# A linear-attention block with two MLPs on one core: the bonus moves from a transposed product to the diagonal of the score tile

## The chip, the cores and the metric

The program runs on one core of a Trainium2 chip. The metric is the device time of one execution in microseconds (us); lower is better. In the profile PE is TensorE's matmuls, PEld its weight loads (each matmul needs one, and they run beside the matmul before them), DVE is VectorE, ACT is ScalarE, POOL is GpSimd, and SP issues the DMA transfers.

## The reference

Four batches of eight heads run a recurrence with a decaying state over 768 steps, and the result goes through two MLPs of width 384 to 2048 to 384.

```python
for t in range(S):                       # S = 768, D = 48
    kt, vt, rt, wt = (k[:, :, t], v[:, :, t], r[:, :, t], w[:, :, t])
    cur = np.einsum('bhd,bhe->bhde', u[None] * kt, vt)
    y[:, :, t] = np.einsum('bhd,bhde->bhe', rt, state + cur)
    state = wt[:, :, :, None] * state + np.einsum('bhd,bhe->bhde', kt, vt)
...
h = x @ w_in;  y1 = (h * np.clip(h + 3.0, 0.0, 6.0) / 6.0) @ w_out
h = y1 @ w_in2;  out = (h / (1.0 + np.exp(-h))) @ w_out2
```

Step t reads the state of the steps before it, and of itself only the "bonus": v at t times the sum over d of r*u*k at t. So in a tile of scores between 128 steps and 128 steps, the entries above the diagonal are decayed products of r and k, and the bonus sums belong on the diagonal.

## The kernel before

**Work.** The sequence is cut into six chunks of 128 steps; a *group* is one chunk of one batch, 24 in all (j is the chunk, g the group). Each group passes through `attention`: VectorE makes running products of the decay forwards and backwards (`pre`, `suf`, lines 600 and 607, with a small reciprocal at 603 between them) and scales r and k by them (`rh`, `kh`, lines 612 and 615). TensorE makes two score tiles `pa` (line 625), each 128 by 4 by 128 for four pairs of heads, and VectorE copies them to SBUF times the mask `causal` (line 636, `a`). `causal` is one above the diagonal and zero on and below it. TensorE also transposes `kh` (line 646, `pk`), ScalarE copies that (650, `khn`), and TensorE makes the chunk's addition to the state (741, `pkv`), which ScalarE or VectorE adds and decays (767; 758 and 759).

**The bonus.** For the groups of the first chunk, VectorE multiplies r by k (line 655, `rkp`) and TensorE sums over d (662, `bb`); for later groups GpSimd makes the products (667 and 670, `ruk`) and VectorE sums them (674). Then `bonus` multiplies v by these sums: three VectorE instructions at lines 685 and 689 into the tile `bv` (the same memory as `ruk`). TensorE adds `bv` to the output in PSUM by three transposing matmuls against the identity (718), after the products of state and scores with r and v (704). ScalarE copies the output `py` to `x` (727).

**MLP blocks.** `block1` and `block2` run per chunk over 16 slices of the hidden width: three groups of products into `h` (821 or 831), an activation, and three groups into an accumulator (842 or 851). Block 0 uses plain f32 products with weights in `val`, which VectorE unpacks from 64-bit words in three steps (32, 38 and 44); the others use f32r products of high and low parts. Attention of chunk j+1 is interleaved with block1 of chunk j.

**Order.** All operations are collected in a `Plan` with a cost in ns for each engine that may run them and a key. `Plan.order` walks through them in planned time, puts next on each engine what can start first, and among equals the lowest key. What comes out is a fixed order for each engine; only semaphores decide the real times. An operation with `port=True` shares one planned resource with GpSimd. `keep_busy` adds products of the identity that nobody reads (`filler`, line 572) with the highest key, so that the plan puts them where TensorE has nothing else to do before the MLPs: 10 pairs planned at 430 ns and 60 at 215 ns.

Of the kernel before, what the change touches and what calls it, by code (L numbers as in the profile page):

```python
# [10 lines left out]
I32 = mybir.dt.int32  # L11
# [333 lines left out]
def tile_decay_attention_mlp2(  # L345
# [109 lines left out]
    def load_w(layer, fc, key, where="wp", after=(), whole=False):  # L455
# [14 lines left out]
        if WW == 2:  # L470
            op({"DVE": 580}, key, lambda e: upper_bits(e, raw.ap, val.ap.bitcast(I32)), [raw], [val])
            for step in (sign_bits, lower_bits):
                op({"DVE": 960}, key, lambda e, step=step: step(e, raw.ap, val.ap.bitcast(I32)),
                   [raw, val], [val], port=True)
# [103 lines left out]
    keep_busy(10, 430)  # L578
    keep_busy(60, 215)
# [8 lines left out]
    def attention(g, key):  # L588
# [14 lines left out]
        op({"DVE": 150}, key, lambda e: e.reciprocal(  # L603
# [8 lines left out]
        op({"DVE": 690}, key, lambda e: e.tensor_tensor(  # L612
            rh.ap, of(rk, 0, NP), pre.ap[:, :, 0:C], op=ALU.mult
        ), [rk, pre], [rh], port=True)
        op({"DVE": 690}, key, lambda e: e.tensor_tensor(
# [14 lines left out]
        o_scores = op({"PE": 900}, key, scores, [kh, rh], pa)  # L630
        if g == 2:
            first_scores.append(o_scores)
        a_sb = []
        for i in range(2):
            a = att("a", [128, NP, C], g, str(i), bufs=2)
            op({"DVE": 690}, key, lambda e, a=a, pa=pa[i]: e.tensor_tensor(  # L636
                a.ap, pa.ap, causal.ap.unsqueeze(1).to_broadcast([128, NP, C]), op=ALU.mult
            ), [pa[i], causal], [a])
            a_sb.append(a)

        if not last:
# [6 lines left out]
            op({"PE": 350}, key, back, [kh, ident], [pk])  # L648
# [3 lines left out]
        ruk = att("ruk", [128, H, D], g)  # L652
        if first:
            rkp = att("rkp", [PD, NP, C], g)
            op({"DVE": 690}, key, lambda e: e.tensor_tensor(
# [9 lines left out]
            op({"PE": 900}, key, sums, [rkp, u_bd], [bb])  # L665
        else:
            op({"POOL": 1000}, key, lambda e: e.tensor_tensor(  # L667
# [9 lines left out]
        bv = Part(ruk.buf, lambda t: flat(ruk).rearrange("p (c a e) -> p c a e", c=KC, e=Q))  # L677
        bv.writes, bv.reads = ruk.writes, ruk.reads

        def bonus(e):  # L680
            b = bb.ap.rearrange("p (a i) x -> p a i x", i=2)
            x = vn.ap.rearrange("p a (n t) -> p a n t", t=T)
            n = Q // T
            for k in range(n):
                e.tensor_tensor(
                    bv.ap[:, 0:2, :, k * T:(k + 1) * T].rearrange("p c a e -> p a c e"),
                    x[:, :, k::n + 3, :], b.to_broadcast([128, NP, 2, T]), op=ALU.mult,
                )
# [402 lines left out]
```

## Time and profile before

| what | value |
|---|---|
| median of three runs | 931.77 us (931.74 to 931.96) |
| profiled execution, its own time | 932.04 us |
| its span, first to last instruction | 930.0 us |
| PE, PEld busy | 922.3 us, 725.1 us |
| DVE, ACT, POOL busy | 575.3 us, 269.3 us, 47.5 us |
| first product of an MLP starts at | 38.40 us |

Busy shares are means over stages. Until 38.40 us the four groups of the first chunk run alone; after that products of the MLPs fill TensorE, and attention of the other twenty groups lies between them until about 441 us. PE's busy time counts products that overlap, and its ends are modelled; whether TensorE waits is better read from the waits and from the spacing of its weight loads.

### The profile page before, as it was taken

To read this page: it belongs to the slowest core of one execution; us is meant where nothing else is said; L and a number is where in the kernel's file an instruction comes from. 1 tells how busy PE (TensorE), PEld (TensorE's weight loads), DVE (VectorE), ACT (ScalarE), POOL (GpSimd) and SP (SyncE) were. 2 spreads that over 40 slices of the span, in tenths; PEclk is the share of its full clock that TensorE was granted. 3 is DMA by queue.
4 is the path that set the end of the run, shared out by engine and by line. 5 is a ranking of instruction groups with operands and counts; after the bars stand their busy time and mean duration, and the time that the engine had idled before them with its cause. 6 is when DMAs were issued, how large, how long until landed. Compare 5 with 4: busy or idle time off the path is not lost.

```text
span 930.0 us, 13728 instructions
## 1 busy us (share of the span) xinstructions
PE 922.3 (99%) x5638; PEld 725.1 (78%) x5638; DVE 575.3 (62%) x998; ACT 269.3 (29%) x496; POOL 47.5 (5%) x52
## 2 busy tenths in 40 slices
PE   9999999999999999999999999999999999999997
PEld 7655457888888888888888888888888888888886
DVE  7998888886676768575449878644543632322221
ACT  2311423222221222121126865422322321211111
POOL 1110001100110010110000000000000000000000
PEclk9999999999999999999999999999999999999999
DMA  9566523321321223120057675554744500100101
GB/s 282 160 206 201 176 57 102 97 74 56 93 58 58 92 68 97 32 88 1 1 193 216 194 228 190 200 174 136 237 136 136 181 23 0 35 1 1 35 0 36
DMA packets 39603, 101.12 MB, mean 109 GB/s; under 512 B 3696, under 2 KB 16112, under 8 KB 39536
## 3 DMA queue, kind: packets, MB, share of 16 engines
q1 hardware_dynamic: 39536, 100.20, 34.1%
q8 instruction: 45, 0.74, 0.3%
q14 instruction: 22, 0.18, 0.1%
HBM read 90.75 MB, written 9.44 MB: 108 GB/s over the span
## 4 chain that ended last, share of the span: by engine, by line
PE 99%; ACT 0%; POOL 0%; issue 0%; POOLq 0%
PE h L831 39%; PE acd L851 21%; PE acc L851 18%; PE h L821 5%; PE acc L842 4%; PE py L704 4%; PE pa L625 3%; PE filler L572 2%; PE py L718 1%; PE pk L646 1%; PE pkv L741 1%; PE bb L662 0%; ACT o L927 0%; ACT x L727 0%; POOL ident masks.py:199 0%
## 5 line engine op out<-in xcount | busy, mean ns | idle before, releaser
L831 PE MATMUL h<-x,w 128*128 128x512 f32 x1584 | 392.6, 391 | 0.0
L831 PEld LDWEIGHTS h<-x,w 128*128 128x128 f32 x1584 | 295.9, 188 | 61.4 <-issue 0.5
L851 PE MATMUL acd<-gh,w 128*128 128x512 f32 x576 | 192.8, 389 | 0.0
L862 DVE CAST gh<-g 128x512 fp32r<-128x512 f32 x146 | 62.5, 428 | 201.0 <-ACT g L921 197.6
L851 PE MATMUL acc<-gh,w 128*128 128x512 f32 x480 | 163.9, 392 | 0.0
L921 ACT ACTIVATE g<-h 128x512 f32<-128x512 f32 x96 | 57.4, 598 | 264.8 <-PE h L831 243.2
L882 ACT ACTIVATE g<-h 128x512 f32<-128x512 f32 x96 | 57.4, 598 | 237.2 <-PE h L831 188.5
L851 PEld LDWEIGHTS acd<-gh,w 128*128 128x128 f32 x576 | 108.1, 188 | 22.4
L864 DVE TENSOR_TENSOR gl<-g,gh 128x512 fp32r<-128x512 f32 x176 | 121.4, 690 | 5.0 <-ACT gh L861 0.8
L884 DVE SCALAR_TENSOR_TENSOR g<-g,h 128x512 f32<-128x512 f32 x96 | 65.9, 686 | 82.5 <-ACT g L882 82.2
L851 PE MATMUL acd<-gl,w 128*128 128x512 f32 x288 | 112.0, 389 | 0.0
L851 PEld LDWEIGHTS acc<-gh,w 128*128 128x128 f32 x480 | 90.1, 188 | 19.1
L851 PE MATMUL acc<-gl,w 128*128 128x512 f32 x240 | 93.5, 390 | 0.0
L851 PEld LDWEIGHTS acd<-gl,w 128*128 128x128 f32 x288 | 54.1, 188 | 11.3
L851 PEld LDWEIGHTS acc<-gl,w 128*128 128x128 f32 x240 | 45.1, 188 | 9.0
L821 PE MATMUL h<-x,val 128*128 128x512 f32 x96 | 44.8, 597 | 0.6 <-ACT x L727 0.6
L842 PE MATMUL acc<-g,val 128*128 128x512 f32 x96 | 43.8, 592 | 0.0
L667 POOL TENSOR_TENSOR ruk<-rkn,u_bc 128x384 f32<-128x384 f32 x20 | 21.0, 1051 | 377.8 <-PE py L718 316.8
L842 PEld LDWEIGHTS acc<-g,val 128*128 128x128 f32 x96 | 17.9, 190 | 21.0 <-issue 19.9
L821 PEld LDWEIGHTS h<-x,val 128*128 128x128 f32 x96 | 17.5, 190 | 19.6 <-issue 18.7
L802 DVE TENSOR_SCALAR_CACHE_REDUCE cval<-cval 128x768 f32<-128x768 f32 x32 | 30.3, 946 | 2.3 <-ACT cval L28 2.3
L636 DVE TENSOR_TENSOR a<-pa,causal 128x512 f32<-128x512 f32 x42 | 27.1, 685 | 7.3 <-PE pa L625 7.3
(106 smaller groups left out, 730.8 us busy)
## 6 DMA issues: line engine op xcount, KB each, us to landing
raw<-in_moe_w_dram SPq DMA_DIRECT2D x32, 768.0 KB, 4.7
craw<-in_moe_w_dram SPq DMA_DIRECT2D x32, 768.0 KB, 4.4
rk<-in_rk_dram SPq DMA_DIRECT2D x21, 448.0 KB, 4.0
rkn<-in_rkn_dram SPq DMA_DIRECT2D x20, 384.0 KB, 3.3
cw<-in_wseq_dram SPq DMA_DIRECT2D x24, 226.2 KB, 2.9
ws<-in_wseq_dram SPq DMA_DIRECT2D x22, 226.2 KB, 2.8
vn<-in_vn_dram SPq DMA_DIRECT2D x22, 224.0 KB, 2.6
x2d<-x SPq DMA_DIRECT2D x18, 256.0 KB, 2.2
```

The source lines that it names most:

```text
L625: e.matmul(pa[i].ap[:, p, :], kh.ap[rows, p, :], rh.ap[rows, p, :], start=True, stop=True,)
L704: e.matmul(py.ap[p * Q:(p + 1) * Q, c, :], lhs, rhs, start=p not in begun, stop=False, skip_group_check=True,)
L802: op({"DVE": 600}, key, lambda e: e.tensor_scalar(val.ap, val.ap, TINY, 0.0, op0=ALU.is_lt, op1=ALU.add, accum_out=stray.ap[:, col:col + 1 ...
L821: op({"PE": 860}, key, lambda e, kc=kc: e.matmul(h.ap, wh.ap[:, 0, kc * 128:(kc + 1) * 128], xh.ap[:, kc, :], start=kc == 0, stop=kc == KC ...
L831: e.matmul(h.ap, a.ap[:, 0, kc * 128:(kc + 1) * 128], b.ap[:, kc, :], start=(kc == 0 and i == 0), stop=(kc == KC - 1 and i == 2),)
L842: op({"PE": 860}, key, lambda e, c=c: e.matmul(acc[c].ap, wh.ap[:, 1, c * 128:(c + 1) * 128], gh.ap, start=fc == 0, stop=fc == FC - 1,), [ ...
L851: e.matmul(acc[c].ap, a.ap[:, 1, sl], b.ap, start=(fc == 0 and i == 0), stop=(fc == FC - 1 and i == 2),)
L862: else e.tensor_copy(gh.ap, src.ap)
L864: op(lo_engs, key, lambda e: e.tensor_tensor(gl.ap, src.ap, gh.ap.bitcast(F32), op=ALU.subtract), [src, gh], [gl], port=True)
L882: op({"ACT": 595}, kk, lambda e, g=g, h=h: e.activation(g.ap, h.ap, AF.Relu, bias=3.0), [h], [g])
L884: op({"DVE": 690}, kk, lambda e, g=g, h=h: e.scalar_tensor_tensor(g.ap, g.ap, 6.0, h.ap, op0=ALU.min, op1=ALU.mult), [g, h], [g])
L921: op({"ACT": 595}, kk, lambda e, g=g, h=h: e.activation(g.ap, h.ap, AF.Silu), [h], [g])
```

## The change

The bonus sums go on the diagonal of the score tile. ScalarE first fills `a` with the identity scaled by the sums, four activations of 128 by 128 for each of the two tiles (`diagonal`); VectorE then copies the scores over it where the mask is not zero (`copy_predicated`) in place of the multiplication by the mask. The product of `a` with v then contains the bonus. The tile `bv`, its three VectorE instructions and the three transposing matmuls of each group are gone. For the first four groups the sums lie in PSUM, and a small activation copies them to SBUF (`bs`); their product and sum get a slightly lower key. The planned costs of several operations are changed, and the filler is 16 pairs planned at 430 ns and 24 at 300 ns.

```diff
-    keep_busy(10, 430)
-    keep_busy(60, 215)
+    keep_busy(16, 430)
+    keep_busy(24, 300)
...
-        for i in range(2):
-            a = att("a", [128, NP, C], g, str(i), bufs=2)
-            op({"DVE": 690}, key, lambda e, a=a, pa=pa[i]: e.tensor_tensor(
-                a.ap, pa.ap, causal.ap.unsqueeze(1).to_broadcast([128, NP, C]), op=ALU.mult
-            ), [pa[i], causal], [a])
...
-            op({"DVE": 690}, key, lambda e: e.tensor_tensor(
+            op({"DVE": 600}, key - 0.05, lambda e: e.tensor_tensor(
                 rkp.ap, of(rk, 0, NP), of(rk, 1, NP), op=ALU.mult
             ), [rk], [rkp], port=True)
...
-        def bonus(e):
...
-        op({"DVE": 880}, key, bonus, [vn, bb], [bv], port=not first)
+        if first:
+            bs = Part(new("ap", "bs", 2, [128, H, 1], f"bs{g}"))
+            op({"ACT": 200}, key, lambda e: e.activation(flat(bs), flat(bb), AF.Copy), [bb], [bs])
+        else:
+            bs = bb
+        a_sb = []
+        for i in range(2):
+            a = att("a", [128, NP, C], g, str(i), bufs=2)
+
+            def diagonal(e, a=a, i=i):
+                for p in range(NP):
+                    e.activation(a.ap[:, p, :], ident.ap, AF.Copy, scale=bs.ap[:, 2 * p + i])
+
+            op({"ACT": 1000}, key, diagonal, [bs, ident], [a])
+            op({"DVE": 610}, key, lambda e, a=a, pa=pa[i]: e.copy_predicated(
+                a.ap, causal.ap.bitcast(I32).unsqueeze(1).to_broadcast([128, NP, C]), pa.ap
+            ), [pa[i], causal], [a])
+            a_sb.append(a)
...
-            for c in range(KC):
-                e.matmul(
-                    py.ap[:, c, :], bv.ap[:, c].rearrange("p a e -> p (a e)"), ident.ap,
-                    start=False, stop=True, is_transpose=True, skip_group_check=True,
-                )
...
-        op({"PE": 1950 if state else 1300}, key, outputs,
-           [*a_sb, vn, bv, ident] + ([rh, state] if state else []), [py])
+        op({"PE": 1700 if state else 1050}, key, outputs,
+           [*a_sb, vn] + ([rh, state] if state else []), [py])
```

The orders move in several places. First VectorE in the opening stage. The names `spare` and `home` are tiles of the first groups kept in space that weights take later; `spare_0_...` holds `pre` and `suf`, `spare_1_...` holds `rh` and `kh`, `spare_2_...` holds `a` and `rkp`. Before, from the start of the fourth group's `pre` to its `rkp`:

```order
L600 SCALAR_TENSOR_TENSOR spare_0_413<-homews,ind 112x516
L685 TENSOR_TENSOR spare_1_357<-home_144,bb_406 128x4x2x16 x2
L689 TENSOR_TENSOR spare_1_357<-home_144,bb_406 128x128
L636 TENSOR_TENSOR spare_2_393<-pa_2_415,causal 128x512
L636 TENSOR_TENSOR spare_2_393<-pa_2_417,causal 128x512
L603 RECIPROCAL indq<-spare_0_413 112x4
L612 TENSOR_TENSOR spare_1_478<-home_159,spare_0_413 112x512
L607 SCALAR_TENSOR_TENSOR spare_0_413<-homews,indq 112x516
L655 TENSOR_TENSOR spare_2_510<-home_159 112x512
L615 TENSOR_TENSOR spare_1_478<-home_159,spare_0_413 112x512
L747 COPY grown_528<-spare_0_413 112x4
```

And in the changed kernel, from the same `pre` to the first step of the second weight slice:

```order
L600 SCALAR_TENSOR_TENSOR spare_0_377<-homews,ind 112x516
L603 RECIPROCAL indq<-spare_0_377 112x4
L612 TENSOR_TENSOR spare_1_398<-home_161,spare_0_377 112x512
L646 TENSOR_TENSOR spare_2_405<-home_161 112x512
L683 COPY_PREDICATED spare_2_316<-causal,pa_2_379 128x512
L683 COPY_PREDICATED spare_2_316<-causal,pa_2_381 128x512
L607 SCALAR_TENSOR_TENSOR spare_0_377<-homews,indq 112x516
L734 COPY grown_469<-spare_0_377 112x4
L32 TENSOR_SCALAR val_0_471<-raw_0_173 128x768
L615 TENSOR_TENSOR spare_1_398<-home_161,spare_0_377 112x512
L38 SCALAR_TENSOR_TENSOR val_0_471<-raw_0_173,val_0_471 128x768
L32 TENSOR_SCALAR val_0_471<-raw_1_175 128x768
```

The three bonus instructions are gone, the two instructions on the scores of the third group stand behind `rkp` of the fourth instead of ahead of its `rh`, and the second unpacking step of the first weight slice (38) has moved ahead of the last scores.

Second, VectorE from the last score copies of the opening stage to the first activation of MLP block 0 (`g_0`), which TensorE needs for its first accumulation. Before:

```order
L636 TENSOR_TENSOR spare_2_510<-pa_3_533,causal 128x512
L636 TENSOR_TENSOR spare_2_510<-pa_3_535,causal 128x512
L38 SCALAR_TENSOR_TENSOR val_0_530<-raw_0_172,val_0_530 128x768
L38 SCALAR_TENSOR_TENSOR val_0_530<-raw_1_178,val_0_530 128x768
L44 SCALAR_TENSOR_TENSOR val_0_530<-raw_0_172,val_0_530 128x768
L44 SCALAR_TENSOR_TENSOR val_0_530<-raw_1_178,val_0_530 128x768
L600 SCALAR_TENSOR_TENSOR pre_617<-ws_433,ind 112x516
L674 TENSOR_REDUCE bb_623<-ruk_543 128x8
L603 RECIPROCAL indq<-pre_617 112x4
L612 TENSOR_TENSOR rh_626<-rk_441,pre_617 112x512
L607 SCALAR_TENSOR_TENSOR suf_632<-ws_433,indq 112x516
L884 SCALAR_TENSOR_TENSOR g_0_630<-g_0_630,h_0_0_615 128x512
```

In the changed kernel (line 871 is the old 884):

```order
L683 COPY_PREDICATED spare_2_405<-causal,pa_3_486 128x512
L683 COPY_PREDICATED spare_2_405<-causal,pa_3_488 128x512
L38 SCALAR_TENSOR_TENSOR val_0_471<-raw_1_175,val_0_471 128x768
L600 SCALAR_TENSOR_TENSOR pre_568<-ws_407,ind 112x516
L44 SCALAR_TENSOR_TENSOR val_0_471<-raw_1_175,val_0_471 128x768
L32 TENSOR_SCALAR val_2_575<-raw_2_519 128x768
L603 RECIPROCAL indq<-pre_568 112x4
L612 TENSOR_TENSOR rh_580<-rk_411,pre_568 112x512
L38 SCALAR_TENSOR_TENSOR val_2_575<-raw_2_519,val_2_575 128x768
L607 SCALAR_TENSOR_TENSOR suf_588<-ws_407,indq 112x516
L44 SCALAR_TENSOR_TENSOR val_2_575<-raw_2_519,val_2_575 128x768
L871 SCALAR_TENSOR_TENSOR g_0_586<-g_0_586,h_0_0_571 128x512
```

Before, four unpacking steps, all of the first weight slices (`val_0`), and the sum `bb_623` stand between the last score copies and `g_0`. Now five steps stand there, two of `val_0` and three of the next pair of slices (`val_2`), and the sum has moved behind `g_0`.

Third, TensorE at the output of the first group of the second chunk. Before:

```order
L741 MATMUL pkv_697<-vn_447,khn_676 48x48 x8
L704 MATMUL py_708<-rh_626,s_111 32x128 x12
L704 MATMUL py_708<-a_4_682,vn_447 32x128 x4
L704 MATMUL py_708<-a_4_689,vn_447 32x128 x4
L704 MATMUL py_708<-a_4_682,vn_447 32x128 x4
L704 MATMUL py_708<-a_4_689,vn_447 32x128 x4
L718 MATMUL py_708<-ident,ruk_543 128x128 x3
L821 MATMUL h_0_3_745<-x_0_0_287,val_2_639 128x512 x3
```

In the changed kernel:

```order
L808 MATMUL h_0_3_673<-x_0_0_281,val_2_575 128x512 x2
L728 MATMUL pkv_680<-vn_422,khn_675 48x48 x8
L696 MATMUL py_690<-rh_580,s_111 32x128 x12
L696 MATMUL py_690<-a_4_618,vn_422 32x128 x4
L696 MATMUL py_690<-a_4_632,vn_422 32x128 x4
L696 MATMUL py_690<-a_4_618,vn_422 32x128 x4
L696 MATMUL py_690<-a_4_632,vn_422 32x128 x4
L808 MATMUL h_0_3_673<-x_0_0_281,val_2_575 128x512
```

The three transposing products are gone, and nothing else in the piece differs but the place in the MLP block at which it stands. Over the whole program the attention pieces between MLP products number 46 before and 43 in the changed kernel (the product of the last check not counted); the commonest output piece was `pkv` then `py` (10 times) and is now `py` then `pkv` (8 times, and 3 times behind a `pk`).

## Rows read from the trace of the kernel before

**Rows 1.** The page's chain that ended last, shares of the span by engine.

```profile
PE 99%; ACT 0%; POOL 0%; issue 0%; POOLq 0%
```

**Rows 2.** All of TensorE's waits: line, releaser: us in total, times, longest.

```profile
PE filler L572 <- POOL ident masks.py:199: 1.4, 1, 1.4
PE h L821 <- ACT x L727: 0.6, 1, 0.6
```

**Rows 3.** Timeline of VectorE over one opening group: start, duration, instruction, [idle before].

```profile
8.91 1.23 DVE L600 TENSOR_TENSOR_SCAN spare<-ws,ind 112x516 f32<-112x516 f32 x1
...
17.93 0.48 DVE L685 TENSOR_TENSOR spare<-vn,bb 128x128 f32<-128x128 f32 x2 [0.91 <-PE bb L662]
19.01 1.29 DVE L636 TENSOR_TENSOR spare<-pa,causal 128x512 f32<-128x512 f32 x2 [0.40 <-PE pa L625]
...
20.30 0.66 DVE L612 TENSOR_TENSOR spare<-home,spare 112x512 f32<-112x512 f32 x1
...
20.88 1.23 DVE L607 TENSOR_TENSOR_SCAN spare<-homews,indq 112x516 f32<-112x516 f32 x1
...
22.02 0.67 DVE L655 TENSOR_TENSOR spare<-home 112x512 f32<-112x512 f32 x1
...
22.61 0.69 DVE L615 TENSOR_TENSOR spare<-home,spare 112x512 f32<-112x512 f32 x1
...
23.28 1.23 DVE L600 TENSOR_TENSOR_SCAN spare<-homews,ind 112x516 f32<-112x516 f32 x1
```

**Rows 4.** The same timeline where GpSimd works beside VectorE.

```profile
27.78 1.39 POOL L667 TENSOR_TENSOR ruk<-rkn,u_bc 128x384 f32<-128x384 f32 x1 [24.45 <-DVE indq L603]
...
28.23 2.03 DVE L607 TENSOR_TENSOR_SCAN spare<-homews,indq 112x516 f32<-112x516 f32 x1
...
30.18 1.42 DVE L655 TENSOR_TENSOR spare<-home 112x512 f32<-112x512 f32 x1
```

**Rows 5.** Timeline of the end of the opening stage, all engines.

```profile
32.19 1.02 DVE L32 TENSOR_SCALAR val<-raw 128x768 int32<-128x768 int32 x2
...
33.91 1.29 DVE L636 TENSOR_TENSOR spare<-pa,causal 128x512 f32<-128x512 f32 x2
...
35.12 1.82 DVE L38 SCALAR_TENSOR_TENSOR val<-raw,val 128x768 int32<-128x768 int32 x2
35.45 0.56 PE L741 MATMUL pkv<-home,spare 128*48 128x48 f32 x16
...
36.26 1.08 PE L704 MATMUL py<-spare,home 128*32 128x128 f32 x32
...
37.86 0.49 ACT L727 ACTIVATE x<-py 128x384 f32<-128x384 f32 x1
38.40 5.42 PE L821 MATMUL h<-x,val 128*128 128x512 f32 x12 [0.58 <-ACT x L727]
```

**Rows 6.** Timeline of the first activation and the first accumulation of block 0.

```profile
41.98 0.66 DVE L884 SCALAR_TENSOR_TENSOR g<-g,h 128x512 f32<-128x512 f32 x1
...
43.66 1.88 PE L842 MATMUL acc<-g,val 128*128 128x512 f32 x4
```

**Rows 7.** Weight-load timeline at an output piece of block 1.

```profile
390.63 0.31 PEld L718 LDWEIGHTS py<-ident,ruk 128*128 128x128 f32 x3 [0.20 <-issue]
390.91 0.19 PEld L851 LDWEIGHTS acc<-gh,w 128*128 128x128 f32 x1
```

**Rows 8.** Timeline of ScalarE: eight small activations scaled per partition, from PSUM.

```profile
21.20 1.73 ACT L767 ACTIVATE s<-pkv,grown 48x48 f32<-48x48 f32 x8 [1.11 <-PE pkv L741]
```

**Rows 9.** Windows of filler's weight loads: stretch, its length, busy (count), PEclk, DMA share, GB/s.

```profile
2.00:7.00 5.00, 3.51 (x24) 1.00 0.94 265
7.60:9.20 1.60, 1.43 (x16) 1.00 1.01 297
```

**Rows 10.** Weight-load timeline of one opening group, `bb` to the next filler.

```profile
16.83 0.97 PEld L662 LDWEIGHTS bb<-u_bd,spare 112*128 112x128 f32 x8
...
19.26 1.07 PEld L572 LDWEIGHTS <-ident 128*128 128x128 bf16 x10
```

More of the change, by code (lines that the diff above doesn't have):

```diff
@@ L470, in load_w @@
         if WW == 2:
-            op({"DVE": 580}, key, lambda e: upper_bits(e, raw.ap, val.ap.bitcast(I32)), [raw], [val])
+            op({"DVE": 480}, key, lambda e: upper_bits(e, raw.ap, val.ap.bitcast(I32)), [raw], [val])
             for step in (sign_bits, lower_bits):
-                op({"DVE": 960}, key, lambda e, step=step: step(e, raw.ap, val.ap.bitcast(I32)),
+                op({"DVE": 870}, key, lambda e, step=step: step(e, raw.ap, val.ap.bitcast(I32)),
                    [raw, val], [val], port=True)
@@ L602, in attention @@
         ), [ws, ind], [pre], port=True)
-        op({"DVE": 150}, key, lambda e: e.reciprocal(
+        op({"DVE": 100}, key, lambda e: e.reciprocal(
             indq.ap[:, 1:SEQ + 1].rearrange("p (a b) -> p a b", b=SEG)[:, :, C:SEG],
@@ L628, in scores @@
                     )
-        o_scores = op({"PE": 900}, key, scores, [kh, rh], pa)
+        o_scores = op({"PE": 1090}, key, scores, [kh, rh], pa)
         if g == 2:
             first_scores.append(o_scores)
-        a_sb = []
-        for i in range(2):
-            a = att("a", [128, NP, C], g, str(i), bufs=2)
-            op({"DVE": 690}, key, lambda e, a=a, pa=pa[i]: e.tensor_tensor(
-                a.ap, pa.ap, causal.ap.unsqueeze(1).to_broadcast([128, NP, C]), op=ALU.mult
-            ), [pa[i], causal], [a])
-            a_sb.append(a)
         if not last:
@@ L663, in sums @@
                              start=True, stop=True)
-            op({"PE": 900}, key, sums, [rkp, u_bd], [bb])
+            op({"PE": 790}, key - 0.05, sums, [rkp, u_bd], [bb])
         else:
+            ruk = att("ruk", [128, H, D], g)
             op({"POOL": 1000}, key, lambda e: e.tensor_tensor(
@@ L676, in attention @@
             ), [ruk], [bb])
-        bv = Part(ruk.buf, lambda t: flat(ruk).rearrange("p (c a e) -> p c a e", c=KC, e=Q))
-        bv.writes, bv.reads = ruk.writes, ruk.reads
-        def bonus(e):
[L681 to L687, printed above, removed]
-                )
-            e.tensor_tensor(
-                bv.ap[:, 2].rearrange("p a (i e) -> p a i e", i=2),
-                x[:, :, n:n + 3:2, :], b.to_broadcast([128, NP, 2, T]), op=ALU.mult,
-            )
-        op({"DVE": 880}, key, bonus, [vn, bb], [bv], port=not first)
+        if first:
[14 more added lines that the diff above has]
+            a_sb.append(a)
         state = states.get(o)
```

8 lines of the change are left out of this document (3 added, 5 removed).

## The prediction

> **What bounds the kernel now.** I read the chain of what ended last first: nearly all of it is TensorE [rows 1]. That alone could be a model's artefact, so the list of TensorE's waits comes next. It has two entries: 1.4 us before the first filler product, and 0.6 us before the first MLP product [rows 2]. After 38.4 us TensorE never waits for another engine, so there a product taken out of its order is time gained and work of the others is hidden. The timeline of the opening stage shows the other regime. There TensorE is busy with filler that nobody reads, and VectorE sets the pace: one group takes it from one `pre` to the next, with waits of 0.91 us (for `bb`) and 0.40 us (for the scores) in it [rows 3]. So the kernel has two parts with different bounds: VectorE's chain up to 38.4 us, TensorE's order after it.
>
> A caution on the first reading. The Trainium skill (Perfetto Trace Analysis, section "Identifying the Most-Contended Engine") says that matmul busy time is a bad measure of TensorE's headroom and that the busy share of the weight loads should be taken. Here that share is 725.1 of 930.0 us, 78%; by that rule a fifth of TensorE is free, the removed products could have been hidden, and the sum below would lose its first term and give about 927.8 us. The waits of this trace do not bear it out: the idle time of a weight load ends with "issue", when the product before it is through [rows 7], and not with another engine.
>
> **The change, part by part.**
>
> *Transposes removed from TensorE.* At an output piece in block 1 the three weight loads of the transposes begin at 390.63 us and the next MLP load at 390.91: 0.28 us [rows 7]. Twenty groups lie after the opening: 20 x 0.28 = 5.6 us. If the 0.20 us of idle ahead of them went too it would be 9.6 us, but I expect such a pause at the new seam, where `py`'s narrow products meet a full-width load. The order also joins pieces differently (43 for 46), which I value at nothing, with 1 us either way. Term 1: -5.6 us (-4.6 to -6.6).
>
> *The opening stage, VectorE.* Per group, from the starts in rows 3: `pre` 1.23, the score pair and the reciprocal 1.29 (19.01 to 20.30), `rh` 0.58, `suf` 1.14, `rkp` 0.59, `kh` with the small copy 0.67; together 5.50 us. The bonus and the waits around it, 2 us more a group, are what disappears: `bb` is now made earlier and feeds ScalarE, and the scores are asked for two instructions later than they were. The second `pre` starts at 8.91 us [rows 3] behind the same seven instructions, reordered. To the last group's score copies there are then three groups' worth, 16.5 us; two first unpacking steps at 0.51 and two others at 0.91 (half of 1.02 and of 1.82) [rows 5], 2.84 us, of which only the 1.02 stood ahead of them before; and the stretch while GpSimd works, where `suf` took 2.03 for 1.23 us and `rkp` 1.42 for 0.67 [rows 3, 4], 1.55 us. GpSimd starts there when its data lands, so I leave it in the same place, though other instructions will meet it. Sum: 8.9 + 20.9 = 29.8 us, against 33.91 [rows 5].
>
> From there to the MLP: the copies 1.29; `py` right behind them (before, `pkv` and filler put it at 36.26, 1.06 after the copies ended); from `py` to `x` 1.60 less the transposes' 0.28; from `x` to the first MLP product 0.54 [rows 5]. That is 33.0 us against 38.4. Term 2: -5.4 us. Without the GpSimd stretch it is -6.9; with one more us of seams -4.4.
>
> *Price of the predicated copy.* The trace shows none. Below, it costs what the masked multiplication does, 0.60 us apiece in the pair above; above, two cycles an element as in the scan, 1.23 us [rows 3]. It reads the same PSUM tile and mask and writes the same tile as the multiplication, so I take 0.60. The upper end would cost 8 x 0.63 = 5.0 us in the opening and nothing behind it, where VectorE is hidden and has lost the bonus.
>
> *Price of the diagonal.* Eight activations of 128 columns scaled per partition. Eight of 48 columns took 1.73 us, 0.216 each [rows 8]; one of 384 columns took 0.49 [rows 5]. On the line between them 128 columns cost 0.28 us, 2.25 us a group. After the opening that is 45 us on an engine with 29% busy, ahead of the scores in its order, and I cost it at nothing. In the opening ScalarE has from the first `bb` (about 8 us) to 29.8 us for 32 of them, 9.0 us, and some 7 us of copies and state additions, so it fits; it would become the pace above (21.8 - 7) / 32 = 0.46 us each. The bounds are 0.22 and 0.49, the upper one costing about 1 us.
>
> *The new wait at the start of block 0.* VectorE is now without slack. From the last score copies at 29.8 to `g_0` stand the copies 1.20, three long unpacking steps 2.73 before `suf` and after it one more 0.91, `pre` 1.23, a short step 0.51, the reciprocal and `rh` 0.67, `suf` 1.14: of the long ones two are on `val_0` and two on `val_2`, so 1.20 + 4 x 0.91 + 1.23 + 0.51 + 0.67 + 1.14 = 8.4 us, and `g_0` ends at 29.8 + 8.4 + 0.66 = 38.9. TensorE's two blocks of `h` take 5.26 us (38.40 to 43.66) [rows 5, 6] and end at 38.2. So its first accumulation waits 0.7 us; before, `g_0` ended at 42.64, a us ahead of need. The queue behind `g_0` is the next unpacking, which TensorE needs 3 us later. Term 3: +0.7 us (0 to 1.2).
>
> *Less filler.* Filler is not read and is off VectorE's chain. But its loads came 0.21 us apart at first (24 in 5.0 us) and 0.10 apart later (16 in 1.6 us) [rows 9]: TensorE runs at half its rate until filler has gone on for some time without a break (1.2 against 2.4 GHz by the spacing; the clock column reads 1.00 in both rows). The changed order puts 24 products there (until 1.4 + 24 x 0.21 = 6.5 us), then `bb`, eight more, then the scores. If the rate has not risen by then, `bb` and `pa` (about 2.0 of the 2.43 us from `bb` to the next filler) [rows 10] take 4.1 and the eight 1.7: scores at 12.3, where VectorE asks for them at about 8.9 + 1.3 + 0.6 = 10.8. Term 4: 0 to +1.5 us; the rate stood low before for longer than these 24 products last, and `bb` is light, so neither end is excluded: +0.8.
>
> *Sum.* -5.6 - 5.4 + 0.7 + 0.8 = -9.5 us. The profiled execution has 932.04 us, so 922.5; it lies 0.3 over the median of the runs, so **922.2 us**. With the terms' ends its own range is 919.5 to 925.
>
> **The rivals.**
>
> *Dear instructions or a slow opening.* Predicated copies at the scan's price give 922.2 + 5.0 = 927.2 us; the activations at their upper bound, or a rate that rises late, 1 to 3 us. For it: the operation is in no row, and ScalarE's margin is 0.46 against 0.28. Against: the same elements through the same ports as a priced instruction.
>
> *A better opening.* The GpSimd stretch falls beside copies from PSUM, no wait at `g_0`, the rate rises early: 922.2 - 1.5 - 0.7 - 0.8 = 919.2 us.
>
> *Nothing comes of it.* Attention's output pieces now need ScalarE, then VectorE, before TensorE's turn, and TensorE waits where it did not: about 0.5 us at each of the 20 groups would eat 10 us, 931.8. Against: the diagonals stand ahead of the scores' arrival in ScalarE's order, and VectorE has 0.7 us a group less to do.
>
> *Slower: TensorE stays at half rate through the opening.* The work of one group at the full rate is 2.43 + 0.56 + 1.08 = 4.07 us [rows 5, 10]; four groups and 80 fillers at 0.106 are 24.8 us. All at half rate: 1.4 + 49.6 + 0.5 = 51.5 us to the first MLP product, 13.1 later than before, and with term 1 the kernel takes 931.8 + 13.1 - 5.6 = 939.3 us. If the rate rises at time t, the opening ends no earlier than 26.0 + t/2: under 33.0 if t is below 14 us, and as late as break-even (44.0) only at 36 us, so it decides only if the rate is low to the end. Against: with these prices TensorE has pauses of less than half a us, since 24.8 of some 31 us is work. The rule that goes this way is in the Trainium skill (TensorE: Matmul & The Clock Gate, Part 1): the low clock is the default, activity releases it and idle gaps bring it back. The trace agrees with its first half [rows 9]; it has no gap to show the second.
>
> **How the numbers follow.** Forecast 0.64; dear or slow opening 0.18 (925 to 930); better opening 0.06; nothing 0.05; slower 0.07. A measurement of this kernel tells about 0.2%, 1.9 us, from no change, so faster holds the first three, 0.88; the same 0.05; slower 0.07. The range 918.8 to 927.4 holds the forecast, the better opening and more than half of the dear one.
>
> **What would show it.** Right: first MLP product near 33 us; VectorE with no `bb` wait; predicated copies near 0.69 us each; the next MLP load 0.2 us behind `py`; waits of TensorE under 2 us after the opening, one of them at `g_0`; filler's loads 0.10 us apart before 12 us. Wrong: TensorE waiting for `a` or for the activations in blocks 0 to 4, ScalarE without pauses in the opening, or filler and scores spaced at the first rate beyond 14 us.

## The result and the profile after

The median of four runs is 922.30 us (922.03 to 923.54), against 931.75 us (931.61 to 931.96) for the kernel before on the same chip: a ratio of 0.9901 [0.9884, 0.9918]. The forecast was 922.2 us. The profiled execution is the slowest of the four, 923.54 us with a span of 921.8; so in the two profiles 8.5 us went, and in the medians 9.45.

The page of the changed kernel, busy time by engine and the chain that ended last (it answers [rows 1]):

```profile
PE 909.6 (99%) x5506; PEld 712.7 (77%) x5506; DVE 572.9 (62%) x935; ACT 317.2 (34%) x683; POOL 60.0 (7%) x52
...
PE 89%; DVE 7%; DMA 3%; issue 0%; ACT 0%; SPq 0%; DVEq 0%
```

TensorE's busy share is 99% as before and tells nothing. The chain tells more: its share there is down from 99% to 89%, and 7% of the span, some 65 us, is now VectorE's. That is not time lost: the chain passes to VectorE where TensorE last waits for `a`, at 96.9 us, and from there back to the start it runs mostly through VectorE and DMA. How much was waited is in the list of TensorE's waits in the changed kernel, in us in total, times, longest (answers [rows 2]):

```profile
PE py L696 <- DVE a L683: 2.4, 2, 1.9
...
PE h L808 <- ACT x L714: 0.7, 1, 0.7
PE bb L653 <- DVE rkp L646: 0.5, 1, 0.5
PE pa L625 <- DVE kh L615: 0.4, 1, 0.4
PE acc L829 <- DVE g L871: 0.3, 1, 0.3
...
```

The wait for `x` was there before. The waits for `rkp` and `kh` lie in the opening. New behind it are 0.3 us for `g_0`, which was forecast, and 2.4 us for `a`, which was not. VectorE over two opening groups (answers [rows 3]):

```profile
9.09 1.22 DVE L600 TENSOR_TENSOR_SCAN spare<-ws,ind 112x516 f32<-112x516 f32 x1
...
11.32 1.34 DVE L683 COPY_PREDICATED a<-causal,pa 128x512 f32<-128x512 int32 x2 [0.21 <-PE pa L625]
...
14.34 1.22 DVE L600 TENSOR_TENSOR_SCAN spare<-homews,ind 112x516 f32<-112x516 f32 x1
15.48 0.67 DVE L615 TENSOR_TENSOR spare<-home,spare 112x512 f32<-112x512 f32 x1
...
18.48 1.31 DVE L683 COPY_PREDICATED spare<-causal,pa 128x512 f32<-128x512 int32 x2
19.69 0.67 DVE L615 TENSOR_TENSOR spare<-home,spare 112x512 f32<-112x512 f32 x1
...
20.36 1.22 DVE L600 TENSOR_TENSOR_SCAN spare<-homews,ind 112x516 f32<-112x516 f32 x1
```

The second of them, from `pre` to `pre`, takes 6.02 us and holds two `kh` (line 615); the first holds none, so they have to be taken together. The two take 11.27 us, with one wait of 0.21 us; before, two took 14.37 [rows 3]. Without that wait a group takes 5.53 us, and 5.50 was forecast. The end of the opening, all engines (answers [rows 5]):

```profile
27.54 1.72 ACT L754 ACTIVATE s<-pkv,grown 48x48 f32<-48x48 f32 x8
27.74 1.82 POOL L659 TENSOR_TENSOR ruk<-rkn,u_bc 128x384 f32<-128x384 f32 x1 [24.40 <-DMA rkn<-in_rkn_dram]
...
28.60 1.35 DVE L683 COPY_PREDICATED spare<-causal,pa 128x512 f32<-128x512 int32 x2
29.28 0.54 ACT L642 ACTIVATE spare<-pk 128x448 f32<-128x448 f32 x1
29.64 1.00 POOL L662 TENSOR_TENSOR ruk<-ruk,rkn 128x384 f32<-128x384 f32 x1
29.83 1.63 DVE L38 SCALAR_TENSOR_TENSOR val<-raw,val 128x768 int32<-128x768 int32 x1
29.88 0.56 PE L728 MATMUL pkv<-home,spare 128*48 128x48 f32 x16 [0.30 <-ACT spare L642]
...
30.54 1.73 ACT L754 ACTIVATE s<-pkv,grown 48x48 f32<-48x48 f32 x8 [0.71 <-issue]
30.70 1.08 PE L696 MATMUL py<-spare,home 128*32 128x128 f32 x32
...
32.29 0.49 ACT L714 ACTIVATE x<-py 128x384 f32<-128x384 f32 x1
...
32.84 5.42 PE L808 MATMUL h<-x,val 128*128 128x512 f32 x12 [0.73 <-ACT x L714]
```

The first MLP product starts at 32.84 us; 33.0 was forecast and 38.40 is before [rows 5]. Two misses cancel in that figure. The last score copies begin at 28.60 instead of 29.8, since 1.55 us had been set aside ahead of them for VectorE's work beside GpSimd. GpSimd's two products now run from 27.74 to 30.64 us, beside the copies and the step behind them, and only that step stretched (the 1.63 us row, 0.68 over the same line undisturbed). From the copies to the product it then takes 4.24 us where 3.15 was worked out: `pkv` stands ahead of `py` on TensorE and waits for ScalarE's copy of `pk` (29.28), which stands behind the state activations of the group before (27.54); and `x` stands behind the eight state activations of 1.73 us. So ScalarE sets the end of the opening, not VectorE. From 13.98 to 29.82 us ScalarE's timeline lists a single pause, of 0.26 us.

Where the time went, by the starts of weight loads in each kernel's profiled execution. "Opening" ends at the first MLP load, "block 0" at the first load of block 1, the rest at the last load; the interval is that of the ratio to the kernel before. The three stage columns are of that one execution, the median is of all runs.

| kernel | median us (range) | opening | block 0 | rest | ratio |
|---|---|---|---|---|---|
| before | 931.77 | 38.40 | 99.2 | 786.1 | |
| changed | 922.30 (922.03 to 923.54) | 32.84 | 101.1 | 781.4 | 0.9901 [0.9884, 0.9918] |
| no_transposes | 924.79 (924.42 to 925.96) | 37.51 | 98.4 | 780.8 | 0.9930 [0.9913, 0.9947] |
| old_filler | 924.51 (923.68 to 925.42) | 34.26 | 100.9 | 781.4 | 0.9924 [0.9908, 0.9941] |
| new_filler_only | 928.60 (927.13 to 936.36) | 33.70 | 99.2 | 786.1 | 0.9984 [0.9963, 1.0005] |
| old_times | 921.82 (921.30 to 922.45) | 32.58 | 99.4 | 781.3 | 0.9897 [0.9881, 0.9914] |
| half_gpsimd | 920.78 (919.36 to 921.01) | 31.88 | 98.6 | 781.9 | 0.9876 [0.9858, 0.9894] |
| pool_1600 | 919.94 (918.64 to 921.07) | 32.05 | 97.9 | 782.5 | 0.9869 [0.9849, 0.9889] |
| old_times_pool_1600 | 920.07 (919.83 to 922.06) | 32.72 | 97.9 | 781.2 | 0.9879 [0.9860, 0.9899] |
| pool_1600_act | 919.49 (918.77 to 921.15) | 31.04 | 99.2 | 781.7 | 0.9866 [0.9847, 0.9885] |
| pool_1600_filler | 921.08 (919.90 to 921.89) | 32.82 | 98.2 | 781.7 | 0.9879 [0.9861, 0.9896] |
| diag_twice | 944.46 (943.16 to 946.58) | 40.23 | 99.1 | 796.0 | 1.0145 [1.0129, 1.0162] |
| diag_twice_later | 937.99 (937.12 to 940.21) | 33.80 | 102.6 | 795.9 | 1.0058 [1.0041, 1.0075] |
| diag_twice_planned | 929.34 (928.83 to 930.29) | 40.81 | 99.7 | 781.5 | 0.9972 [0.9960, 0.9983] |

From before to the changed kernel: opening -5.6, block 0 +1.9, rest -4.7 us.

### The profile page after: what moved, and what is told of

It is laid out like the page before. It is cut to its first block, busy times and chain, and to the rows that moved or that the text cites. A ratio compares the mean times of both kernels' runs of the same rounds, so it can differ in the third digit from the quotient of the medians.

```text
span 921.8 us, 13563 instructions
## 1 busy us (share of the span) xinstructions
PE 909.6 (99%) x5506; PEld 712.7 (77%) x5506; DVE 572.9 (62%) x935; ACT 317.2 (34%) x683; POOL 60.0 (7%) x52
## 4 chain that ended last, share of the span: by engine, by line
PE 89%; DVE 7%; DMA 3%; issue 0%; ACT 0%; SPq 0%; DVEq 0%
PE h L818 39%; PE acd L838 21%; PE acc L838 18%; PE py L696 3%; DMA raw<-in_moe_w_dram 3%; PE pa L625 2%; PE acc L829 2%; PE h L808 2%; DVE val L38 1%; DVE val L44 1%; PE pkv L728 1%; PE pk L638 1%; DVE suf L607 1%; DVE val L32 1%; DVE pre L600 1%; DVE a L683 0%
## 5 line engine op out<-in xcount | busy, mean ns | idle before, releaser
L849 DVE CAST gh<-g 128x512 fp32r<-128x512 f32 x152 | 66.7, 439 | 198.5 <-ACT g L908 194.2
L851 DVE TENSOR_TENSOR gl<-g,gh 128x512 fp32r<-128x512 f32 x176 | 124.7, 709 | 4.5
L680 ACT ACTIVATE a<-ident,bb 128x128 f32<-128x128 f32 x160 | 49.7, 390 | 7.0 <-DVE bb L666 7.0
L659 POOL TENSOR_TENSOR ruk<-rkn,u_bc 128x384 f32<-128x384 f32 x20 | 31.9, 1595 | 299.3 <-DVE bb L666 255.3
L683 DVE COPY_PREDICATED a<-causal,pa 128x512 f32<-128x512 int32 x42 | 28.9, 731 | 10.9 <-PE pa L625 10.9
```

The lines of the kernel that those rows point to most:

```text
L659: op({"POOL": 1000}, key, lambda e: e.tensor_tensor(ruk.ap, of(rkn, 0, H), u_bc.ap, op=ALU.mult), [rkn, u_bc], [ruk], port=True)
L680: e.activation(a.ap[:, p, :], ident.ap, AF.Copy, scale=bs.ap[:, 2 * p + i])
L683: op({"DVE": 610}, key, lambda e, a=a, pa=pa[i]: e.copy_predicated(a.ap, causal.ap.bitcast(I32).unsqueeze(1).to_broadcast([128, NP, C]), pa.ap
L849: else e.tensor_copy(gh.ap, src.ap)
L851: op(lo_engs, key, lambda e: e.tensor_tensor(gl.ap, src.ap, gh.ap.bitcast(F32), op=ALU.subtract), [src, gh], [gl], port=True)
```

## The experiments

### The transposes alone

**no_transposes**: the kernel before, without the three products.

```diff
-            for c in range(KC):
-                e.matmul(
-                    py.ap[:, c, :], bv.ap[:, c].rearrange("p a e -> p (a e)"), ident.ap,
...
```

> The kernel before without the three transposing products of each group (the bonus is then missing from the output; VectorE still computes it, and order and filler stay as they were). My theory: the seam after py is 0.28 us shorter for each of the 20 later groups and nothing else moves: 5.6 us, plus 0.3 at the end of the opening, 925.5 to 926.5 us. Rival: weight loads leave a fifth of TensorE free and hide them: 931 us or more.

Measured 924.79 us, 6.6 less than the kernel before on the same chip (931.41). Between the profiled executions it is 7.0 us: 5.3 in the rest, 0.8 in block 0, 0.9 in the opening. The rest holds 16 groups, so 0.33 us a group where [rows 7] gave 0.28. The changed kernel got 4.7 there. Weight loads at the seam behind `py` in the changed kernel (answers [rows 7]):

```profile
400.32 0.90 PEld L696 LDWEIGHTS py<-a,vn 128*32 128x32 f32 x32
401.42 0.53 PEld L818 LDWEIGHTS h<-x,w 128*128 128x128 f32 x3 [0.20 <-issue]
```

The 0.20 us pause has moved from the transposes to the MLP's load, as forecast. The Trainium skill (Perfetto Trace Analysis, "Identifying the Most-Contended Engine") judges TensorE's headroom by MFU, the share of its peak rate that is used, and by the busy share of the weight loads. Read by that share alone, 78%, a fifth of TensorE would have been free and nothing gained; this run speaks against that reading, since taking 0.28 us of loads away gave a little more than 0.28.

### The filler alone, in both directions

**old_filler**: the changed kernel with the old filler, as below. **new_filler_only**: the same lines the other way, in the kernel before.

```diff
-    keep_busy(16, 430)
-    keep_busy(24, 300)
+    keep_busy(10, 430)
+    keep_busy(60, 215)
```

> The changed kernel with the filler of before (10 pairs planned at 430 ns, 60 at 215). My theory: the opening is set by VectorE's chain, so filler that is not read changes it by less than 1.5 us: first MLP product at 32 to 34 us, 921.5 to 923.5 us in all; its loads rise to the upper rate once and stay there. Rival: fewer idle products made TensorE free earlier and gave a good part of the opening's gain; then the first MLP product comes at 35 us or later and the time is 925 us or more.

> The kernel before with the changed filler alone (16 pairs planned at 430, 24 at 300). With the changed work the old filler cost about 2 us (924.5 for 922.3), because filler stands ahead of the last state product and of the output in TensorE's queue. My theory: here too the last output starts up to 1 us earlier: 930 to 931.2 us. Rival: the pauses it leaves let TensorE's rate fall at the start of the MLP, 932 us or more.

old_filler takes 924.51 us, 2.2 more than the changed kernel. In the profiled executions the opening is 1.4 us longer and the rest the same. TensorE at the end of the opening:

```profile
29.48 1.69 PE L572 MATMUL filler<-ident 128*128 128x256 bf16 x14
31.10 0.56 PE L728 MATMUL pkv<-home,spare 128*48 128x48 f32 x16
31.60 1.08 PE L696 MATMUL py<-spare,home 128*32 128x128 f32 x32
32.61 1.92 PE L572 MATMUL filler<-ident 128*128 128x256 bf16 x16
34.37 1.88 PE L808 MATMUL h<-x,val 128*128 128x512 f32 x4
```

Fourteen filler products stand ahead of `pkv`, and sixteen between `py` and the first MLP product. TensorE takes its products in the order that the plan fixed, so real work whose inputs are there waits for products nobody reads; no view calls that a wait, since TensorE is busy.

new_filler_only shows more. VectorE's order in the opening is that of before, bonus and all, but one group now reads (VectorE's timeline):

```profile
14.80 1.23 DVE L600 TENSOR_TENSOR_SCAN spare<-homews,ind 112x516 f32<-112x516 f32 x1
16.07 0.49 DVE L685 TENSOR_TENSOR spare<-vn,bb 128x128 f32<-128x128 f32 x2
...
17.16 1.29 DVE L636 TENSOR_TENSOR spare<-pa,causal 128x512 f32<-128x512 f32 x2 [0.40 <-PE pa L625]
...
21.43 1.23 DVE L600 TENSOR_TENSOR_SCAN spare<-homews,ind 112x516 f32<-112x516 f32 x1
```

The wait of 0.91 us for `bb` [rows 3] is gone with nothing but filler taken away, and the group takes 6.63 us. The opening ends at 33.70 us in this execution, the fastest of its ten. Of the 4.7 us, 2.4 are VectorE's waits for `bb` and the scores, and 1.55 come from GpSimd, whose products now run beside the bonus and the score copies and no longer stretch a `suf` and an `rkp` [rows 4]. So the larger part of the 5.6 us in the opening can be had without the bonus's move, and the two changes don't add up.

It can't be had reliably. Its ten runs lie between 927.13 and 936.36 us, and time goes with the granted clock: 0.999 in the first, 0.990 in the last, and the others stand in nearly the same order by both. 0.009 of 934 us is 8.4 us, nearly the 9.2 between them. Hence the median of 928.60, not told from before.

### Planned times and GpSimd

**old_times**: the changed kernel, with the planned costs of before for all that both kernels contain.

```diff
-            op({"DVE": 480}, key, lambda e: upper_bits(e, raw.ap, val.ap.bitcast(I32)), [raw], [val])
+            op({"DVE": 580}, key, lambda e: upper_bits(e, raw.ap, val.ap.bitcast(I32)), [raw], [val])
...
-        o_scores = op({"PE": 1090}, key, scores, [kh, rh], pa)
+        o_scores = op({"PE": 900}, key, scores, [kh, rh], pa)
...
```

> The changed kernel with the planned times of before for every operation that both have, 690 ns for the predicated copy, and the changed filler. My theory: planned times move instructions but neither remove VectorE's work nor TensorE's products, so most of the gain stays: 921.5 to 925 us, first MLP product at 32 to 35 us. Rival: the new planned times made the opening tight; then the first MLP product is at 36 us or later and the time 926 us or more.

921.82 us, 0.5 less than the changed kernel, ranges overlapping: the times taken from the trace brought nothing. But block 0 is 1.7 us shorter, and part of it ran at the lower clock. In this execution the granted clock was 0.50 from 33 to 36 us, and the first MLP products took 7.11 us where the same twelve took 5.42 in the changed kernel:

```profile
32.58 7.11 PE L808 MATMUL h<-x,val 128*128 128x512 f32 x12 [1.38 <-ACT x L714]
```

Without these 1.7 us its block 0 would be 97.7 us (an estimate from the two rows). That points at what block 0 lost. One of VectorE's scans, `suf`, in the stretch from 33 to 145 us, count, busy us and mean ns; first in the changed kernel:

```profile
L607 DVE TENSOR_TENSOR_SCAN suf<-ws,indq 112x516 f32<-112x516 f32 x7 | 10.4, 1481 | 0.0
```

and with the old planned times:

```profile
L607 DVE TENSOR_TENSOR_SCAN suf<-ws,indq 112x516 f32<-112x516 f32 x7 | 8.6, 1227 | 0.0
```

A scan takes 1.22 us alone. In the changed kernel some take 2.02, beside GpSimd's products. VectorE, GpSimd and TensorE around the longest wait, cut:

```profile
70.89 2.02 DVE L607 TENSOR_TENSOR_SCAN suf<-ws,indq 112x516 f32<-112x516 f32 x1
...
71.91 2.72 POOL L662 TENSOR_TENSOR ruk<-ruk,rkn 128x384 f32<-128x384 f32 x1
...
75.15 0.86 PE L696 MATMUL py<-rh,s 112*32 112x128 f32 x24 [1.86 <-DVE a L683]
```

GpSimd's own products stretch too, 2.72 us for one. Summed over that stretch, by how much each VectorE instruction exceeds the median of its line (counting 0.15 us or more), VectorE lost 7.7 us in the changed kernel, 3.5 in old_times and 2.7 before. Two kernels test whether GpSimd is the cause, both made from the changed one.

**half_gpsimd**: the second product on 8 elements a partition instead of 384, in the same order, so the later groups' bonus is left out in part. **pool_1600**: both products planned at what they take.

```diff
-                ruk.ap, ruk.ap, of(rkn, 1, H), op=ALU.mult
+                ruk.ap[:, 0:1, 0:8], ruk.ap[:, 0:1, 0:8], of(rkn, 1, H)[:, 0:1, 0:8], op=ALU.mult
```

```diff
-            op({"POOL": 1000}, key, lambda e: e.tensor_tensor(
+            op({"POOL": 1600}, key, lambda e: e.tensor_tensor(
...
```

> The changed kernel, its order untouched, with GpSimd's second product of each later group cut to 8 of 384 columns (the bonus of those groups is then wrong), so GpSimd works half as long. My theory: the new waits of TensorE in block 0 (2.7 us in the profile of the changed kernel) come from VectorE's instructions that are stretched while GpSimd works beside them (7.7 us there, against 2.7 before). Then the stretch falls to 4 us or less, the wait for the scores of 1.9 us to under 0.6, block 0 from 101.1 to 99 to 100 us, and the time to 920 to 921.8 us. Rival: the waits come from the order or from ScalarE's queue; block 0 stays above 100.7 us and the time above 922.

> The changed kernel with GpSimd's products planned at 1600 ns, what they took after the change, in place of 1000. My theory: the plan then keeps VectorE's port-sharing work out of their way and block 0 loses its waits: 920 to 922 us. Rival: the order's waits are not GpSimd's, and another order is as good or bad: 922 to 924 us.

With half of GpSimd's work and the order unchanged, block 0 is 2.4 us shorter, VectorE's loss is 4.4 us and the wait for `a` shrinks. It does not vanish (TensorE's waits):

```profile
PE py L696 <- DVE a L683: 1.0, 2, 0.5
```

With the true price, block 0 is 3.1 us shorter, the loss is 4.4 us again, the wait for `a` is gone from the list, and the kernel takes 919.94 us. (In the profiles 0.8 us more of the gain lies in the opening, where the clock did not fall in this execution.) So most of the new waits in block 0 come from GpSimd's products beside VectorE's in the order of the changed kernel. The price of 1.0 us does not make that order by itself: old_times plans GpSimd at 1.0 us too, and its list has no wait for `a`. Either set of prices moves the scans out of the way.

**old_times_pool_1600** is old_times with that price too.

> The changed work with the planned times of before, which had no waits in block 0 at 921.8 us, and GpSimd planned at 1600 ns. My theory: planned times choose among orders that differ by a us or two, with no trend: 920 to 923 us. Rival: true planned times add up to a better order; then this one, true for GpSimd alone, lies with the changed kernel or above it, 922.3 or more.

920.07 us, block 0 97.9: with GpSimd's price right, the other planned times still make no difference.

### The price of the diagonal

**diag_twice** writes each diagonal twice, **diag_twice_later** only behind the first chunk, and **diag_twice_planned** is the first with the plan told so.

```diff
             def diagonal(e, a=a, i=i):
-                for p in range(NP):
...
+                for _ in range(2):
+                    for p in range(NP):
...
-            op({"ACT": 1000}, key, diagonal, [bs, ident], [a])
+            op({"ACT": 2440}, key, diagonal, [bs, ident], [a])
```

In diag_twice the last two lines are as they were; in diag_twice_later the loop is over `range(1 if first else 2)`.

> The changed kernel with every diagonal written twice (eight more activations per group, same result). After the change eight took 2.45 us, 0.31 each; twice that is 0.61, over the 0.46 at which ScalarE becomes the pace of the opening. My theory: the opening grows by 32 x 0.15 = 4.8 us, first MLP product at 36 to 39 us, and after it ScalarE has room: 926 to 928.5 us. Rival one: hidden everywhere, 923.5 us or less. Rival two: ScalarE's queue stands ahead of TensorE in the MLP blocks as well, 931 us or more.

> The changed kernel with the diagonal written twice only for the 20 later groups, order untouched. Doubled everywhere, blocks 1 to 5 became 14.6 us longer (796.0 for 781.4), though ScalarE was busy under half of them; block 0 did not. My theory: the eight more activations stand in ScalarE's queue ahead of an MLP activation that TensorE needs within some 4 us, so each late group loses about 0.9 us there, whatever the opening did: opening 32 to 33.5 us, blocks 1 to 5 again near 796, 935 to 939 us. Rival: the loss was carried over from the late opening and the low rate in it; then 923 to 927 us.

> The diagonal written twice for all groups, and planned at 2440 ns a tile instead of 1000, so the order knows of it. Theory one, position: what was lost in blocks 1 to 5 was the place in the queue, ScalarE has time enough; the plan then moves the activations and blocks 1 to 5 return to within 3 us of 781.4, with the opening still late (36 to 40 us): 926 to 932 us. Theory two, ScalarE's time itself: blocks 1 to 5 stay above 790 us and the time above 938.

diag_twice takes 944.46 us: 7.4 more in the opening, and 14.6 more in the rest, where the second copies were to cost nothing. My theory of a free ScalarE fell there, though ScalarE is busy for 46 of the 100 us from 140 on. diag_twice_later has 14.5 us of them behind an opening of 33.8, so they aren't carried over from the opening. It shows how they arise (its timeline):

```profile
160.02 4.79 ACT L681 ACTIVATE a<-ident,bb 128x128 f32<-128x128 f32 x16
...
164.72 0.57 ACT L870 ACTIVATE g<-h 128x512 f32<-128x512 f32 x1
...
164.91 0.55 DVE L666 TENSOR_REDUCE bb<-ruk 128x8 f32<-128x384 f32 x1 [1.57 <-ACT a L681]
...
167.57 0.66 DVE L852 TENSOR_TENSOR gl<-g,gh 128x512 fp32r<-128x512 f32 x1
...
168.29 0.50 PE L839 MATMUL acc<-gl,w 128*128 128x512 f32 x1 [0.28 <-DVE gl L852]
```

Sixteen diagonals stand ahead of the MLP's activation `g` in ScalarE's queue for 4.79 us, and VectorE stands 1.57 us behind them at the next `bb`; `g` is late, then `gl`, then TensorE's accumulation. A scan of 1.53 us beside GpSimd stands ahead of this `gl` too. Twelve such waits of TensorE for `gl` add up to 3.6 us in its list, and three for `g` to 3.2; in the weight loads' list those of blocks 1 to 5 for `gl`, `g` and `gh` are 16 us, and the changed kernel has none of them. diag_twice_planned does the same work in the same number of instructions, in an order that knows its length, and the rest is 781.5 us again, as in the changed kernel. Not ScalarE's time but the diagonals' place in its queue was the cost there.

In the opening the plan that knows of it does not hide it: 40.81 us, with a granted clock of 0.50 from 36 to 40 us in that execution. 32 more activations at 0.305 us are 9.8 us of ScalarE. The clock fell in diag_twice's opening as well (window: length, busy PE, PEld, DVE, ACT, POOL with counts, PEclk, DMA share, GB/s):

```profile
24.00:33.00 9.00, 9.00 (x92) 7.26 (x85) 7.75 (x12) 8.38 (x31) 3.13 (x2) 0.50 0.42 130
```

ScalarE is busy for 8.38 of these 9 us, and TensorE is at 1.2 GHz, the lower of its two levels. The score products' loads, 0.97 us at the upper level, took 1.68 in the changed kernel in such a stretch. How much of the 7.4 us is the clock's, the run does not tell.

### Towards a better kernel

**pool_1600_act** plans GpSimd at 1600 and the diagonal at 1220 ns, as measured; **pool_1600_filler** is pool_1600 with more filler.

```diff
-            op({"ACT": 1000}, key, diagonal, [bs, ident], [a])
+            op({"ACT": 1220}, key, diagonal, [bs, ident], [a])
```

```diff
-    keep_busy(24, 300)
+    keep_busy(36, 240)
```

> The changed kernel with GpSimd planned at 1600 ns and the diagonal at 1220 ns a tile, what four activations took, in place of 1000. Theory: the plan is truer, the order as good as with GpSimd alone corrected (919.9 us): 918.5 to 921 us. Rival: orders differ by chance; 921 to 924 us.

> The changed kernel with GpSimd planned at 1600 ns and 36 filler pairs planned at 240 ns in place of 24 at 300. Theory: executions differ by up to 2.4 us because TensorE's rate falls back in the opening in some of them; more filler keeps it up, so the spread shrinks to under 1.2 us, and its place in the queue costs under 1.5 us: 919.5 to 921.5 us. Rival: the spread has another source and stays at 2 us or more.

pool_1600_act has the lowest median of all, 919.49 us: 2.8 below the changed kernel, and the four runs of the one don't overlap those of the other. Against pool_1600 its 0.45 us can't be told from nothing. More filler did not narrow the runs: they spread over 2.0 us, and the median is 1.1 higher. That theory fell.

## Why the prediction held, step by step

**Term 1, the transposes, -5.6 us: right.** Alone they are worth 5.3 us in the rest and 0.8 in block 0. In the changed kernel the rest gave 4.7; that the joining of the pieces took the difference is not shown.

**Term 2, the opening, -5.4 us: right in size, half right in cause.** The step "VectorE sets the pace" and that "the bonus and the waits around it" disappear took VectorE's waits for `bb` and `pa` as the bonus's. new_filler_only has the bonus and not the wait for `bb`. TensorE was late because it sat in filler. The filler stands right behind the scores in [rows 10]; I read a TensorE busy with it as a free one. The new work alone, with the old filler, ends the opening at 34.26 us, the new filler alone at 33.70, both at 32.84.

VectorE's part of the sum came: 5.53 us a group for 5.50. The end of the opening did not: there the pace is ScalarE's. The step "so it fits" counted "some 7 us of copies and state additions" beside the diagonals up to 29.8 us. For three groups and the fourth's copy of `pk` they are 8.8 us in the trace of before, and 9.5 in the changed one with `bs`; the diagonals are 9.8 for 9.0; ScalarE is busy for 19.3 of the 21.8 us, and what TensorE needs from it comes late.

**Term 4, less filler, +0.8 us: wrong in sign.** The step is "Filler is not read and is off VectorE's chain". Under the new work, less filler is worth 2.2 us, since filler stands in TensorE's order ahead of real work; that was put at nothing. The fear behind the term was that the rate would not have risen by `bb`. It had: `bb`'s loads took 0.97 us. But the clock fell again behind them. Weight loads in two stretches of the changed kernel, the second just behind the fall: length, busy (count), PEclk, DMA share, GB/s:

```profile
7.80:8.60 0.80, 0.69 (x9) 1.00 0.94 249
9.30:11.10 1.80, 1.60 (x16) 0.52 1.10 295
```

The score products' loads took 1.68 us for 0.97. Ahead of them TensorE's loads had been idle twice in 3 us (weight-load timeline):

```profile
6.89 0.97 PEld L653 LDWEIGHTS bb<-u_bd,rkp 112*128 112x128 f32 x8 [0.75 <-DVE rkp L646]
...
9.22 1.68 PEld L625 LDWEIGHTS pa<-rh,kh 48*128 48x128 f32 x16 [0.66 <-DVE kh L615]
```

VectorE lost only 0.21 us by it, at 11.32, since it was itself some 0.3 us behind the schedule I had worked out. TensorE and ScalarE lost more. half_gpsimd has the same order in the opening, and in its execution the clock did not fall. The first group's `pkv` in the changed kernel, then in half_gpsimd, and there the end of the opening:

```profile
13.32 0.56 PE L728 MATMUL pkv<-vn,khn 128*48 128x48 f32 x16
```

```profile
11.48 0.56 PE L728 MATMUL pkv<-vn,khn 128*48 128x48 f32 x16
...
28.32 0.54 ACT L642 ACTIVATE spare<-pk 128x448 f32<-128x448 f32 x1
...
31.88 5.42 PE L808 MATMUL h<-x,val 128*128 128x512 f32 x12 [0.73 <-ACT x L714]
```

From ScalarE's copy of `pk` to the first MLP product it is 3.56 us in both, so the difference of 0.96 us arose before: 0.24 of it is there at the second `pre` (9.09 and 8.85), where the data had landed later, and the rest, 0.7, comes with the fall, since nothing else differs ahead of GpSimd's products. In diag_twice_later, with that order again, the clock was 0.50 for longer (8 to 13 us) and the opening ends at 33.80. So the term had two parts: the clock cost about what was forecast for it, and filler ahead of real work, between executions without a fall, 2.4 us (34.26 and 31.88).

The Trainium skill (TensorE: Matmul & The Clock Gate, Part 1) has idle gaps bring the low clock back. The fall here follows two idle stretches, 0.75 and 0.66 us; half_gpsimd's loads were idle for 0.61 and 0.66 us at the same two places without a fall, so these gaps alone don't decide, and the cause of the fall stays open.

**Term 3, the wait at the start of block 0, +0.7 us: mis-sized.** At `g_0` it is 0.3. But block 0 grew by 1.9 us although no_transposes is 0.8 shorter there, so the new waits are 2.7 us: 2.4 for `a` and the 0.3. "VectorE is now without slack" was right; I asked what that does to the next activation, and not what GpSimd's stretch, which I had priced in the opening, does in block 0 with the slack gone.

**Prices.** The predicated copy was taken at 0.60 us, by the spacing of a pair; the diagonal at 0.28 an activation. The changed kernel's groups, ScalarE's and VectorE's:

```profile
L680 ACT ACTIVATE a<-ident,bb 128x128 f32<-128x128 f32 x160 | 49.7, 390 | 7.0 <-DVE bb L666 7.0
L683 DVE COPY_PREDICATED a<-causal,pa 128x512 f32<-128x512 int32 x42 | 28.9, 731 | 10.9 <-PE pa L625 10.9
```

A pair of copies takes 1.31 to 1.35 us where the masked multiplication took 1.29, and the instruction behind it starts 1.21 to 1.25 us after the pair (18.48 to 19.69, 28.60 to 29.83), 0.60 to 0.63 each: the forecast was right, and the scan's 1.23 is refuted. Eight diagonals take 2.44 us, 0.31 each, since the instructions overlap and their mean of 390 ns is not their spacing. **"I cost it at nothing"** of the diagonals after the opening holds at this price, but "an engine with 29% busy" is no reason: at twice the price it cost 14.6 us until the plan knew it.

**The sum.** -5.6 - 5.4 + 0.7 + 0.8 = -9.5 us were forecast. In the profiles the opening gave -5.6 where terms 2 and 4 said -4.6, block 0 +1.9 where terms 1 and 3 said -0.4, the rest -4.7 where term 1 said -4.5. The opening was 1.0 better and block 0 2.3 worse, and partly they cancel; the profiled execution is the highest of its four, so the medians came nearer still, -9.45. That 922.2 met 922.30 so closely is luck; the bulk of it, terms 1 and 2, is not. Of the rivals, neither the dear instructions nor half rate throughout came, nor a wait at every group. Of the better opening one condition came, GpSimd beside the copies from PSUM; the rate rose early but fell again, and `g_0` was waited for. Its size came in other kernels, pool_1600_act's 31.04 us. Two of the signs named for being wrong did show: TensorE waited for `a` in block 0, and ScalarE was almost without pauses in the opening from 14 us on; the waits after the opening are 2.7 us where less than 2 was named.

## What to carry to other kernels

Work that nobody reads is not free on an in-order engine: to see whether it delays real work, ask what stands in the queue between a product's inputs and its start, since the wait lists show a busy engine. A plan's price that is too low shows up far from the instruction itself, on whatever stands behind it in the queue; when an engine loses its slack, price again every stretch that the slack had covered. And take a term's cause apart by making each half of the change alone, in both kernels: a total that comes out right hides terms that cancel. Before two profiles are compared stage by stage, look at the granted clock of the stage in each.

## What was unexpected about the hardware

VectorE and GpSimd slowed each other in both directions: scans from 1.22 to 2.02 us, unpacking steps from 0.95 to 1.63 (and 0.94 in the same place of half_gpsimd, where GpSimd's second product is cut to 0.21 us), GpSimd's products from 1.0 us (new_filler_only, beside the bonus and the score copies, which kept their times) to 2.72. At the end of the opening the predicated copies from PSUM (28.60 us above) kept their 1.35 us a pair too, and the unpacking step behind them stretched.

And ten executions of new_filler_only, whose opening is thinly filled, differed by 1% with the granted clock, 0.990 to 0.999, with nothing else changed; the kernel before spread over 931.17 to 934.06 us in thirteen runs on the same chip. One order of the opening ran, in three profiles, without a fall of the clock, with a short one and with a longer one.
